# Two-part first query load, a later second query load, half of the first key products on GpSimd, and new engine orders in an attention-plus-MLP kernel

## The chip, the cores and the metric

The kernel runs on one core of one Trainium2 chip. The metric is the device time of one execution in microseconds (us). Three executions of the kernel before took 103.77, 103.62 and 103.83 us; their median is 103.77 us.

## What is computed

Four batches of four heads, 1088 tokens, head dimension 32: a linear attention with a degree-two polynomial sketch, followed by a two-layer MLP with a `h - tanh(h)` activation. The attention output is the MLP's input, 4352 tokens of 128 features.

```python
def phi(x):
    a = np.einsum('rd,bhsd->bhsr', S1, x)          # r = 8
    b = np.einsum('rd,bhsd->bhsr', S2, x)
    return np.einsum('bhsi,bhsj->bhsij', a, b).reshape(*x.shape[:-1], r * r)
q_p, k_p = (phi(q), phi(k))
kv = np.einsum('bhsf,bhsd->bhfd', k_p, v)
z = np.sum(k_p, axis=2)
num = np.einsum('bhsf,bhfd->bhsd', q_p, kv)
den = np.einsum('bhsf,bhf->bhs', q_p, z)[..., None] + 1e-06
x = (num / den) ...                                 # to (4352, 128)
h = x @ w_in                                        # d_ff = 2048
out = (h - np.tanh(h)) @ w_out
```

## The kernel before

Each batch's tokens stand in 34 columns of 32 tokens. The program records named operations; five lists in `ORDERS` say, word for word, in which order each engine (TensorE, ScalarE, VectorE, GpSimd, and SyncE, which issues nearly all loads and stores) runs them. `SESSIONS` says in which order the users of each PSUM bank follow each other, and each pair `a<b` in `GATES` makes operation a wait for operation b. Nothing is reordered at run time: an instruction that waits holds all that stands behind it on its engine.

**Attention, keys (batch b).** `kT` turns the raw keys in 32x32 blocks (VectorE, line 542), `kp` multiplies them with the sketch weights (TensorE, 553), `kab` turns the result back (VectorE, 559). `wk` are the products of the two sketches (573), cut by `KCUTS` into pieces for VectorE and GpSimd. For batch 0, `kap0` (ScalarE, 563) first copies one factor to PSUM, so that VectorE's pieces read one operand from there. `gram` (584), `gm` (590) and `fold` (593) give the key sums folded with S2: `fold0` needs `gm0` and `s2f` (532), and `wq0u` (ScalarE, 597) copies its result out. `sum` (609), `kvz` (619), `turn` (629), `ndw` (636) make the matrices that queries are weighed with.

**Attention, queries (chunk u).** There are five chunks: 12 and 22 columns of batch 0, and then one of 34 for each further batch. `qT` turns the raw queries (656), `qp` and `qpu0` multiply (679 for chunk 0, 700), `qab` copies them out (ScalarE 691 for chunk 0, VectorE 706), `au`, `dn`, `rd`, `an` (711 to 717) form the denominator and the scaled factor, `qm` the products (724, on VectorE and GpSimd), `qt` their turned form (731), `num` weighs them (TensorE, 746) and `x` writes the MLP's input xT (769).

**MLP.** Ten groups of 256 to 512 tokens. For each of 16 blocks of w_in a group has `h` (TensorE, 829 or 838), `t` = tanh (ScalarE, 832 or 841; three PSUM banks in turn, or pairs of banks in groups 7 to 9), and `o` (TensorE, 889 or 854), which accumulates tanh against w_out. The part without tanh is added as xT against `w_in @ w_out`, which is formed once: `wT` transposes w_in by DMA (SyncE, 782), `wp` multiplies (787), `whi`/`wlo` split it (791, 792), `lin` applies it (881). `out` turns a result (894) and SyncE stores it (901). Operation h17 is block 1 of group 1: 16 operations make a group.

**Casts.** `wic0` to `wic3` cast the four quarters of w_in (775; the last on GpSimd), `woc0` to `woc2` the parts of w_out (778, GpSimd).

**Filler.** TensorE's list also has matmuls whose result nobody reads: `~` (256 columns in a 32-wide strip, line 424), `*`, `!`, `$` (512 columns) and `^` (256 columns), line 416. `!` waits for `qab1`, `$` for `wqu0`.

Of the kernel before, what the change touches and what calls it, by code (L numbers as in the profile page):

```python
# [271 lines left out]
ORDERS = {
    "tensor": """
~52 sk ~17 kp0 sk2 *4 ^1 gram0 qp0 fold0 *2 ^1 qpu0 sum0.0 sum0.4 qp1 turn0 $2 num0.0 num0.1 !1 h0 h1 h2 o0 h3 o1 h4
o2 h5 o3 kp1 h6 h7 h8 h9 o4 h10 gram1 o5 h11 o6 h12 fold1 o7 h13 o8 h14 o9 h15 num1.0 num1.1 o10 o11 o12 h30 h22 h20
wp h19 h18 h32 h31 o13 o14 h47 o15 h24 lin0.whi h16 lin0.wlo h17 qp2 h42 h23 lin1.whi h25 lin1.wlo o16 o17 h21 o18 o19
h29 o20 h28 h27 o21 o22 o23 h26 o24 o25 h34 h39 o26 o27 h38 o28 h43 kp2 h33 o29 o30 h35 o31 h46 h45 gram2 lin2.whi h40
fold2 lin2.wlo sum1.0 h36 h44 o32 o33 o34 turn1 o35 h37 h41 o36 num2.0 num2.1 o37 o38 o39 o40 o41 o42 h51 h49 o43 o44
o45 o46 h48 o47 h53 h64 qp3 h50 h57 lin3.whi h52 lin3.wlo o48 h59 h54 o49 o50 h55 h65 o51 o52 o53 h63 h56 o54 h58 o55
h60 h62 o56 o57 h61 o58 h66 o59 h68 sum2.0 h67 h69 o60 turn2 h74 h70 o61 o62 h72 o63 h73 num3.0 num3.1 h76 lin4.whi  # L280
h71 lin4.wlo h78 h79 o64 o65 o66 h77 o67 o68 o69 h85 h75 h80 o70 kp3 h84 o71 h83 o72 h109 gram3 o73 h87 o74 fold3 h88
h101 o75 o76 o77 h82 o78 h81 h86 o79 h103 qp4 lin5.whi h91 lin5.wlo o80 o81 h90 o82 h89 o83 o84 h108 h94 o85 o86 o87
o88 h92 o89 o90 h93 h97 o91 o92 h95 h105 sum3.0 h98 h96 o93 o94 o95 turn3 h111 h100 h110 lin6.whi lin6.wlo o96 o97 o98
h99 h104 num4.0 num4.1 h102 h106 h107 o99 o100 h116 h112 h113 o101 o102 o103 h117 h114 o104 o105 h115 h119 h118 o106
o107 o108 o109 o110 o111 h123 h122 h121 h125 h120 lin7.whi h124 lin7.wlo h129 o112 o113 o114 h128 o115 h126 o116 o117
h127 o118 h130 o119 h135 h134 h131 o120 o121 o122 h133 o123 h132 h141 o124 o125 o126 o127 h140 h136 h137 h139 h138
lin8.whi lin8.wlo o128 o129 o130 o131 o132 h144 h145 h147 h146 o133 o134 h142 h143 h149 h148 o135 o136 h150 o137 o138
h152 o139 h151 o140 o141 h153 o142 o143 lin9.whi h154 h155 lin9.wlo o144 h157 h156 o145 o146 o147 o148 h158 o149 h159
o150 o151 o152 o153 o154 o155 o156 o157 o158 o159
""",  # L290
    "scalar": """
k0.1 s1 act0 kap0 wq0u qab0 wic0 kvz0 ndw0 wic1 wic2 x0.0 t0 t1 t2 t3 t4 t5 t6 t7 t8 t9 t10 t11 t12 t13 t14 t15 x1.0
x1.2 t30 t22 t20 t19 t32 t18 t31 t47 t24 t17 t16 t42 t23 t25 t21 t29 t28 t27 t26 t34 t39 t38 t43 t33 t46 t35 t45 t40
kvz1 t36 t44 ndw1 t37 t41 t51 t49 t48 t53 t64 t50 t57 t52 t59 t54 t55 t65 t63 t56 t58 t60 t62 t61 t66 t68 kvz2 t67 t69
t70 ndw2 t74 t73 t72 t76 t71 t78 t79 t77 t75 t80 t85 t84 t83 t109 t87 t88 t101 t82 t103 t81 t86 t91 t90 t89 t94 t108
t92 t93 t97 t95 t105 kvz3 t96 t98 ndw3 t111 t110 t99 t100 t104 t102 t107 t106 t112 t116 t114 t118 t122 t120 t124 t128
t126 t134 t130 t132 t140 t138 t136 t144 t146 t148 t142 t150 t152 t154 t156 t158 out9.1 st9
""",
    "vector": """
hm4 hm4.0 hm4.1 hm4.2 hm4.3 sel bmask hm2 kT0.2 wkm kT0.0 wq wq0 qT0.0 kab0 qT0.12 s2f gm0 wk0.0 wk0.8 wk0.16 au0 dn0  # L300
wqu0 rd0 an0 qm0.0 qt0.0 qt0.2 qab1 au1 dn1 rd1 an1 kT1.2 kT1.0 qm1.0 kab1 qt1.2 gm1 qt1.0 wqu1 wk1.0 whi wlo wk1.24
qT1.0 out0 qab2 kT2.2 dn2 rd2 kT2.0 kab2 out1 gm2 qt2.2 wqu2 qt2.0 wk2.0 wk2.24 x2.0 x2.2 qT2.0 out2 qab3 qT3.0 dn3
rd3 qt3.2 qt3.0 out3 x3.2 x3.0 kT3.0 kT3.2 kab3 gm3 wk3.0 wk3.24 wqu3 out4 qab4 dn4 rd4 qt4.0 out5 qt4.2 x4.0 x4.3
x4.2 out6 out7 out8 out9.0
""",
    "gpsimd": """
id0 id1 au1.0 kTz0 qTz0 vz1 identb au1.1 kTz1 wqz vz0 wk0.22 wk0.29 qm0.2 qTz1 wic3 woc0 qm1.2 woc1 woc2 wk1.30 wk1.12
au2 an2 qm2.2 qm2.0 wk2.30 au3 wk2.12 an3 qm3.2 qm3.0 wk3.12 au4 wk3.30 an4 qm4.0 qm4.2
# [684 lines left out]
```

## Time and profile before

| what | us |
|---|---|
| median of three executions | 103.77 |
| the profiled execution, as timed | 104.69 |
| its span, first to last instruction | 101.8 |
| TensorE busy | 93.5 (92% of the span) |
| ScalarE busy | 78.5 (77%) |
| VectorE busy | 54.8 (54%) |
| GpSimd busy | 34.7 (34%) |
| chain that ended last: share on TensorE | 68% |
| the same: VectorE, GpSimd, DMA | 13%, 7%, 4% |

The span is cut into instructions with their start and duration on each engine. "Idle before" names what an engine waited for. The chain that ended last is followed back from the last instruction, at each step to what released it. Matmuls overlap: one of 512 columns is recorded with 0.38 us, but six in a row take 1.46 us, so that the spacing of two starts, 0.216 us, and not the duration, is what one costs in a row.

### The profile page before, as it was taken

What the parts mean: (1) busy time and instruction counts of PE and PEld (TensorE: products, weight loads), DVE (VectorE), ACT (ScalarE), POOL (GpSimd) and SP (SyncE); (2) the same over time, 40 slices, a digit from 0 to 9 for tenths busy, and PEclk for the clock granted to TensorE, in tenths of its full rate; (3) what the DMA queues carried; (4) which work ended last, traced back from release to release, by engine and by line L of the source; (5) the groups of instructions that cost most, each with busy time, mean ns of one, the idle gap of its engine ahead of it and who ended that gap; (6) DMA issues with size and microseconds to landing.
All of it is one profiled execution on the core that took longest, in us unless ns stands there. A gap on an engine that the chain in (4) does not pass through costs nothing.

```text
span 101.8 us, 3175 instructions
## 1 busy us (share of the span) xinstructions
PE 93.5 (92%) x1358; PEld 48.7 (48%) x1370; DVE 54.8 (54%) x95; ACT 78.5 (77%) x156; POOL 34.7 (34%) x42
## 2 busy tenths in 40 slices
...
GB/s 57 362 246 278 348 336 160 283 114 241 6 243 221 10 189 139 0 78 182 90 72 181 65 6 0 0 144 36 10 40 37 6 0 79 76 0 58 65 51 100
DMA packets 25966, 11.74 MB, mean 115 GB/s; under 512 B 19808, under 2 KB 24416, under 8 KB 25952
## 3 DMA queue, kind: packets, MB, share of 16 engines
...
q10 hardware_dynamic: 328, 0.40, 1.4%
q8 instruction: 10, 0.16, 0.8%
...
HBM read 8.79 MB, written 2.23 MB: 108 GB/s over the span
## 4 chain that ended last, share of the span: by engine, by line
PE 68%; DVE 13%; POOL 7%; DMA 4%; issue 2%; SPq 1%; ACT 1%; DVEq 0%; POOLq 0%
PE ps L889 23%; PE ps L838 16%; PE ps L829 8%; PE ps L746 6%; POOL qp L724 4%; DMA qraw<-in_q_dram 4%; PE ps L881 3%; DVE qpT L731 2%; PE ps L700 2%; PE ps L609 2%; DVE qab L706 2%; PE ps L553 2%; PE ps L854 2%; DVE wk L573 2%; POOL wk L573 1%
## 5 line engine op out<-in xcount | busy, mean ns | idle before, releaser
L841 ACT ACTIVATE tt<-ps 128x512 bf16<-128x512 f32 (+2 forms) x112 | 52.5, 552 | 8.4 <-PE ps L838 4.2
L889 PE MATMUL ps<-tt,w_out 128*128 128x512 bf16 (+3 forms) x141 | 39.0, 355 | 0.5 <-ACT tt L841 0.3
L838 PE MATMUL ps<-xT,w_in 128*128 128x512 bf16 (+2 forms) x107 | 32.7, 353 | 2.0 <-ACT tt L841 0.7
L889 PEld LDWEIGHTS ps<-tt,w_out 128*128 128x128 bf16 x144 | 13.9, 98 | 12.8 <-issue 1.4
L832 ACT ACTIVATE tt<-ps 128x1024 bf16<-128x1024 f32 (+2 forms) x24 | 18.4, 860 | 0.5
L838 PEld LDWEIGHTS ps<-xT,w_in 128*128 128x128 bf16 x112 | 9.9, 97 | 16.9 <-ACT tt L841 11.0
L724 POOL TENSOR_TENSOR qp<-an,qab 128x1152 f32<-128x1152 f32 (+2 forms) x8 | 15.4, 1925 | 3.6 <-DVE an L717 3.1
L731 DVE STREAM_TRANSPOSE qpT<-qp 128x1152 f32<-128x1152 f32 (+2 forms) x10 | 11.2, 1128 | 8.6 <-POOL qp L724 8.6
L894 DVE STREAM_TRANSPOSE osb<-ps 128x512 f32<-128x512 f32 (+3 forms) x9 | 5.9, 657 | 17.5 <-PE ps L889 17.0
L573 POOL TENSOR_TENSOR wk<-kab 128x384 f32<-128x384 f32 (+2 forms) x8 | 9.0, 1126 | 18.6 <-PE ps L889 18.1
L829 PE MATMUL ps<-xT,w_in 128*128 128x512 bf16 (+2 forms) x48 | 12.1, 335 | 0.1
L746 PE MATMUL ps<-qpT,ndw 32*32 32x288 f32 (+4 forms) x320 | 6.9, 352 | 0.4 <-DVE qpT L731 0.3
L829 PEld LDWEIGHTS ps<-xT,w_in 128*128 128x128 bf16 x48 | 4.5, 98 | 4.6 <-ACT tt L832 1.2
L542 DVE STREAM_TRANSPOSE kT<-kraw 128x512 f32<-128x512 f32 (+1 forms) x8 | 5.6, 718 | 0.8 <-DMA kraw<-in_k_dram 0.8
L656 DVE STREAM_TRANSPOSE qT<-qraw 128x1088 f32<-128x1088 f32 (+2 forms) x5 | 5.3, 1065 | 1.1 <-DMA qraw<-in_q_dram 1.1
L706 DVE STREAM_TRANSPOSE qab<-ps 128x1152 f32<-128x1152 f32 (+1 forms) x4 | 5.1, 1272 | 1.4 <-PE ps L700 1.4
L711 POOL TENSOR_TENSOR au<-qab 128x288 f32<-128x288 f32 x3 | 2.4, 790 | 9.9 <-DVE qab L706 7.0
L769 DVE CAST xT<-ps 128x576 bf16<-128x576 f32 (+2 forms) x7 | 4.4, 684 | 2.5 <-PE ps L746 2.5
L746 PEld LDWEIGHTS ps<-qpT,ndw 32*32 32x32 f32 x320 | 4.0, 103 | 3.2 <-DVE qpT L731 2.0
L609 PE MATMUL ps<-wk,vx 128*32 128x64 f32 x288 | 4.8, 220 | 0.0
L609 PEld LDWEIGHTS ps<-wk,vx 128*32 128x32 f32 x288 | 4.2, 110 | 0.7 <-issue 0.7
L559 DVE STREAM_TRANSPOSE kab<-ps 128x576 f32<-128x576 f32 x4 | 3.1, 769 | 2.7 <-PE ps L553 2.7
...
## 6 DMA issues: line engine op xcount, KB each, us to landing
...
vx<-in_v_dram SPq DMA_DIRECT2D x8, 128.0 KB, 3.3
...
```

The costliest lines, as they stand in the source:

```text
L573: P.op(f"wk{b}.{n0}", eng, (dve if eng == "vector" else pool)(64 * n), lambda e, n0=n0, n1=n1, n=n, a_=a_: e.tensor_tensor(out=wk[0][:, n0 ...
L609: ins = e.matmul(ps[32 * h:32 * h + 32, SB, 0:64], vx[i][:, h, t, :], wk[0][:, 4 * t + h, :], start=(t == 0), stop=(t == 8), tile_position ...
L706: P.op(f"qab{u}", "vector", dve(32 * n), lambda e: e.transpose(out=qab[ui][:, 0:n, :].rearrange("p (h t) x -> p h t x", h=H), in_=ps[:, b0 ...
L724: P.op(f"qm{u}.{h0}", eng, (pool if eng == "gpsimd" else dve)(64 * (n1 - n0)), lambda e, n0=n0, n1=n1, b_=b_: e.tensor_tensor(out=qp[ui][: ...
L731: P.op(f"qt{u}.{h0}", "vector", dve(64 * (n1 - n0)), lambda e, n0=n0, n1=n1: e.transpose(out=qpT[ui][:, n0:n1, :, :].rearrange("p n y j -> ...
L746: ins = e.matmul(ps[32 * h:32 * h + 32, ct, 0:32 * own[ct]], ndw[i][32 * ct:32 * ct + 32, y, 32 * h:32 * h + 32], qpT[ui][32 * ct:32 * ct ...
L829: P.op(f"h{s + y}", "tensor", pe(n), lambda e, jb=jb, b0=b0, y=y: e.matmul(ps[:, b0 + y, 0:n], w_in[:, 128 * (jb + y):128 * (jb + y) + 128 ...
L832: P.op(f"t{s}", "scalar", act(2 * n), lambda e, ts=ts, b0=b0: e.activation(out=tt[:, ts:ts + 2, 0:n], in_=ps[:, b0:b0 + 2, 0:n], func=AF.T ...
L838: P.op(f"h{s}", "tensor", pe(n), lambda e, jb=jb, bk=bk: e.matmul(ps[:, bk, 0:n], w_in[:, 128 * jb:128 * jb + 128], xT[:, t0:t0 + n], star ...
L841: P.op(f"t{s}", "scalar", act(n), lambda e, ts=ts, bk=bk: e.activation(out=tt[:, ts, 0:n], in_=ps[:, bk, 0:n], func=AF.Tanh, scale=-1.0), ...
L889: P.op(f"o{slot + jb}", "tensor", pe(n), lambda e, jb=jb, ts=ts: e.matmul(acc[:, 0:n], w_out[:, jb, :], tt[:, ts, 0:n], start=late and jb ...
L894: P.op(f"out{g}", "vector", dve(n), lambda e: e.transpose(out=osb[u][:, 0:n], in_=acc[:, 0:n]), r=ka, w=[("osb", u)], prio=when)
```

## The change

- The first batch's queries are loaded in two parts (columns 0 to 11, then 12 to 33) instead of three. The first part is issued right behind the keys, the second behind the values and ahead of w_in.
- `KCUTS` for batch 0 gives VectorE three pieces of 6 (18 of 36) and GpSimd two of 9 (18 of 36); before, VectorE had 22 and GpSimd 14.
- `s2f` is four small ScalarE operations (line 530 of the new file) instead of one on VectorE.
- All five orders, the bank sessions and the gates are new.

```diff
-KCUTS = ((('vector', 0, 8), ('gpsimd', 22, 29), ('vector', 8, 16), ('gpsimd', 29, 36), ('vector', 16, 22)), (('gpsimd', 12, 24), ('vector', 0, 12), ('vector', 24, 30), ('gpsimd', 30, 36)), (('gpsimd', 12, 24), ('vector', 0, 12), ('vector', 24, 30), ('gpsimd', 30, 36)), (('gpsimd', 12, 24), ('vector', 0, 12), ('vector', 24, 30), ('gpsimd', 30, 36)))
+KCUTS = ((('vector', 0, 6), ('gpsimd', 18, 27), ('vector', 6, 12), ('gpsimd', 27, 36), ('vector', 12, 18)), (('gpsimd', 12, 24), ('vector', 0, 12), ('vector', 24, 30), ('gpsimd', 30, 36)), (('gpsimd', 12, 24), ('vector', 0, 12), ('vector', 24, 30), ('gpsimd', 30, 36)), (('gpsimd', 12, 24), ('vector', 0, 12), ('vector', 24, 30), ('gpsimd', 30, 36)))
...
-WENG = ()
+WENG = ('s2f',)
 SKB = 6
 WOC = ((0, 4), (4, 8), (8, 16))
+Q0 = ((0, 384), (384, 1088))
...
     "tensor": """
-~52 sk ~17 kp0 sk2 *4 ^1 gram0 qp0 fold0 *2 ^1 qpu0 sum0.0 sum0.4 qp1 turn0 $2 num0.0 num0.1 !1 h0 h1 h2 o0 h3 o1 h4
+~43 *1 sk ~4 sk2 ~16 kp0 *5 gram0 qp0 fold0 *1 ^1 qpu0 sum0.0 sum0.4 *2 turn0 qp1 $1 num0.0 num0.1 !1 h1 h11 h9 h10 h5 h0
...
     "gpsimd": """
-id0 id1 au1.0 kTz0 qTz0 vz1 identb au1.1 kTz1 wqz vz0 wk0.22 wk0.29 qm0.2 qTz1 wic3 woc0 qm1.2 woc1 woc2 wk1.30 wk1.12
-au2 an2 qm2.2 qm2.0 wk2.30 au3 wk2.12 an3 qm3.2 qm3.0 wk3.12 au4 wk3.30 an4 qm4.0 qm4.2
+qTz0 kTz0 id0 id1 au1.0 vz1 kTz1 vz0 qTz1 wk0.27 wk0.18 au1.1 wqz qm0.2 wic3 woc0 qm1.2 woc1 woc2 wk1.30 wk1.12 au2
+an2 qm2.0 qm2.2 wk2.30 wk2.12 au3 an3 qm3.0 qm3.2 wk3.30 identb wk3.12 au4 an4 qm4.2 qm4.0
...
 GATES = """
-id0<hm4.3 kTz0<hm4.3 kTz1<qT0.0 vz0<sel au1.0<bmask au1.1<bmask wqz<kp0 qTz0<hm4 qTz1<wq0 vz1<wq v1.0<o11 v1.1<h25
+id1<hm4.2 kTz1<qT0.0 vz0<sk2 au1.0<kT0.2 au1.1<qpu0 wqz<wqu0 s1<hm4.0 k0.0<kTz0 v1.0<t16 v1.1<kT2.0 v1.2<dn2 v1.3<t17
...
-    load_q(0, 0, 256, L + 2, 0)
+    for x, (lo, hi) in enumerate(Q0):
+        load_q(0, lo, hi, L + 2 + 3 * x, x)
     load_v(0, "sync", L + 3)
     load_w_in(0, L + 5)
     load_w_in(1, L + 6)
-    load_q(0, 256, 640, L + 8, 1)
     load_w_in(2, L + 8.5)
     load_w_in(3, L + 9)
-    load_q(0, 640, S, L + 10, 2)
```

VectorE before, from the turn of batch 0's key sketches (`kab0`) to the products of chunk 0 (`qm0.0`); the row with 704 columns is the second part of batch 0's queries being turned:

```order
L559 STREAM_TRANSPOSE kab<-ps 128x18x2x16
L656 STREAM_TRANSPOSE qT<-qraw 128x704
L532 TENSOR_TENSOR s2f<-ps,bmask 128x128
L590 TENSOR_TENSOR gm<-ps,bmask 128x32
L573 TENSOR_TENSOR wk<-ps,kab 128x512 x2
L573 TENSOR_TENSOR wk<-ps,kab 128x384
L711 TENSOR_TENSOR au<-qab,ps 128x12x8
L713 TENSOR_REDUCE dn<-au 128x12
L599 TENSOR_REDUCE wq<-ps 128x8
L715 RECIPROCAL rd<-dn 128x12
L717 TENSOR_TENSOR an<-ps,rd 128x96
L724 TENSOR_TENSOR qp<-an,ps 128x384
```

The same stretch of VectorE now:

```order
L560 STREAM_TRANSPOSE kab<-ps 128x18x2x16
L446 TENSOR_REDUCE bmask<-ident 128x4
L526 COPY wq<-ps 128x4x16
L591 TENSOR_TENSOR gm<-ps,bmask 128x32
L574 TENSOR_TENSOR wk<-ps,kab 128x384 x3
L712 TENSOR_TENSOR au<-qab,ps 128x12x8
L714 TENSOR_REDUCE dn<-au 128x12
L600 TENSOR_REDUCE wq<-ps 128x8
L716 RECIPROCAL rd<-dn 128x12
L718 TENSOR_TENSOR an<-ps,rd 128x96
L657 STREAM_TRANSPOSE qT<-qraw 128x704
L725 TENSOR_TENSOR qp<-an,ps 128x384
```

The 704-column turn went from ahead of `gm0` to between `an0` and `qm0.0`, `s2f` left the engine, two small operations came in, and the key products shrank from 1408 to 1152 elements a partition.

SyncE's opening before (kraw are keys, qraw queries, vx values; 128x1088 is a whole batch):

```order
L918 DMA s<-in_S_dram 8x4x32
L466 DMA kraw<-in_k_dram 128x576
L472 DMA qraw<-in_q_dram 128x384
L472 DMA qraw<-in_q_dram 128x256
L472 DMA qraw<-in_q_dram 128x448
L489 DMA vx<-in_v_dram 32x4x288 x2
L489 DMA vx<-in_v_dram 32x4x256 x2
L495 DMA w_in_f<-in_moe_w_in_dram 128x512 x4
L500 DMA w_out_f<-in_moe_w_out_dram 128x4x128
L466 DMA kraw<-in_k_dram 128x1088
L500 DMA w_out_f<-in_moe_w_out_dram 128x4x128
L500 DMA w_out_f<-in_moe_w_out_dram 128x8x128
```

And now:

```order
L919 DMA s<-in_S_dram 8x4x32
L467 DMA kraw<-in_k_dram 128x576
L473 DMA qraw<-in_q_dram 128x384
L490 DMA vx<-in_v_dram 32x4x256 x2
L490 DMA vx<-in_v_dram 32x4x288 x2
L473 DMA qraw<-in_q_dram 128x704
L496 DMA w_in_f<-in_moe_w_in_dram 128x512 x4
L467 DMA kraw<-in_k_dram 128x1088
L501 DMA w_out_f<-in_moe_w_out_dram 128x4x128 x2
L501 DMA w_out_f<-in_moe_w_out_dram 128x8x128
L473 DMA qraw<-in_q_dram 128x1088
L783 DMA_TRANSPOSE w_inT<-w_in 128x16x128
```

The columns that chunk 0 needs now come in one load instead of two; the rest of batch 0's queries moved behind the values; batch 1's keys and queries moved ahead (the queries stood behind the transposing DMA `wT`).

VectorE before, around batch 1's keys and chunk 1, from `an1` on:

```order
L717 TENSOR_TENSOR an<-qab,rd 128x192
L542 STREAM_TRANSPOSE kT<-kraw 128x2x8x32
L542 STREAM_TRANSPOSE kT<-kraw 128x2x9x32
L724 TENSOR_TENSOR qp<-an,qab 128x768
L559 STREAM_TRANSPOSE kab<-ps 128x18x2x16
L731 STREAM_TRANSPOSE qpT<-qp 128x768
L590 TENSOR_TENSOR gm<-ps,bmask 128x32
L731 STREAM_TRANSPOSE qpT<-qp 128x768
L599 TENSOR_REDUCE wq<-ps 128x8
L573 TENSOR_TENSOR wk<-kab 128x768
```

The same stretch now:

```order
L718 TENSOR_TENSOR an<-qab,rd 128x192
L725 TENSOR_TENSOR qp<-an,qab 128x768
L543 STREAM_TRANSPOSE kT<-kraw 128x2x9x32
L543 STREAM_TRANSPOSE kT<-kraw 128x2x8x32
L732 STREAM_TRANSPOSE qpT<-qp 128x768 x2
L560 STREAM_TRANSPOSE kab<-ps 128x18x2x16
L574 TENSOR_TENSOR wk<-kab 128x384
L574 TENSOR_TENSOR wk<-kab 128x768
L657 STREAM_TRANSPOSE qT<-qraw 128x1088
L591 TENSOR_TENSOR gm<-ps,bmask 128x32
```

Chunk 1's products and their turns went ahead of batch 1's `kab1`, and `gm1` went behind both `wk1` pieces and the turn of batch 1's queries.

82 lines of the change are left out of this document (41 added, 41 removed).

## The prediction

> **What bounds the kernel now.** First the busy time by stage. I cut the span where the MLP starts, where its first group ends, and where the last attention work ends.
>
> ```profile
> core 0: us, PE busy (x) PEld busy (x) DVE busy (x) ACT busy (x) POOL busy (x), PEclk, DMA share, GB/s
> 0.00:14.30 14.30, 11.72 (x311) 7.88 (x314) 10.35 (x31) 5.16 (x11) 6.43 (x21) 1.00 0.91 268
> 14.30:23.20 8.90, 8.04 (x129) 3.63 (x129) 7.20 (x13) 7.00 (x18) 3.70 (x3) 1.00 0.95 200
> 23.20:78.00 54.80, 53.08 (x787) 26.11 (x795) 33.69 (x46) 46.40 (x101) 24.55 (x18) 1.00 0.38 92
> 78.00:98.70 20.70, 20.61 (x134) 11.08 (x132) 3.26 (x6) 19.70 (x28) 0.00 (x0) 1.00 0.24 38
> PE ps L838 <- ACT tt L841: 0.4, 2, 0.2
> PE ps L746 <- DVE qpT L731: 0.3, 1, 0.3
> ```
>
> From 23.2 us on TensorE lacks 1.72 + 0.09 = 1.8 us of being busy all the time, and the change takes no matmul out of it. (The last two lines, of the waits from 23.2 to 98.7, name 0.7 us of it.) The third stage can give at most 1.8 us. The rest is a delay: whatever makes the MLP start or its first group end earlier moves the end as far, unless later waits grow. What sets that start is read in the chain that ended last:
>
> ```profile
> 2.06 4.20 DMA qraw<-in_q_dram
> 6.35 0.58 DVE qT L656
> 6.93 0.66 DVE kab L559
> 8.66 1.66 DVE wk L573 x3
> 10.32 0.17 DVE au L711
> 11.08 0.27 DVE an L717
> 11.37 0.56 DVE qp L724
> ```
>
> Loads, then VectorE without a pause: `qT0.0` waits for the queries until 6.35, and `kab0` stands behind it. TensorE's timeline shows what these hold:
>
> ```profile
> 0.77 2.96 PE L424 MATMUL ps<-const-bfloat16-1.0 128*32 128x256 bf16 x52 [0.77 <-PEq L978]
> 4.04 0.73 PE L424 MATMUL ps<-const-bfloat16-1.0 128*32 128x256 bf16 x17
> 5.07 0.72 PE L553 MATMUL ps<-kT,wkm 64*32 64x288 f32 x16 [0.31 <-DVE kT L542]
> 7.65 0.38 PE L584 MATMUL ps<-kab 128*32 128x32 f32 x18 [0.43 <-DVE kab L559]
> 8.71 0.41 PE L593 MATMUL ps<-gm,s2f 128*128 128x32 f32 x2 [0.19 <-DVE gm L590]
> 14.34 0.66 PE L838 MATMUL ps<-xT,w_in 128*128 128x384 bf16 x3 [0.57 <-ACT xT L769]
> 21.36 1.25 PE L746 MATMUL ps<-qpT,ndw 32*32 32x192 f32 x64
> 81.29 1.46 PE L889 MATMUL ps<-tt,w_out 128*128 128x512 bf16 x6
> ```
>
> **Term 1, the start of the MLP: -0.6 us.** These rows give the prices:
>
> ```profile
> qraw<-in_q_dram SPq DMA_DIRECT2D x1, 192.0 KB, 3.2
> qraw<-in_q_dram SPq DMA_DIRECT2D x1, 128.0 KB, 4.2
> 7.52 0.87 DVE L656 STREAM_TRANSPOSE qT<-qraw 128x704 f32<-128x704 f32 x1
> 7.63 0.40 ACT L563 COPY ps<-kab 128x288 f32<-128x288 f32 x1 [4.33 <-DVE kab L559]
> 9.16 0.19 ACT L597 COPY wq<-ps 128x32 f32<-128x32 f32 x1 [1.13 <-PE ps L593]
> L573 POOL TENSOR_TENSOR wk<-kab 128x384 f32<-128x384 f32 x3 | 2.5, 847 | 6.8 <-PE ps L889 6.7
> L573 POOL TENSOR_TENSOR wk<-kab 128x448 f32<-128x448 f32 x2 | 1.9, 958 | 0.2 <-POOL vx L450 0.2
> ```
>
> The new first query load is the 192 KB size, in that load's place: there by about 4.8 instead of 6.26 (2.06 + 4.20). `kT0.0` is done at 5.0 (`kp0` starts on it at 5.07, as now), `qT0.0` (0.58) and one small operation fit before `kp0` ends at 5.79, so `kab0` starts at 5.83 instead of 6.85 and ends at 6.57. Behind it TensorE has five fillers of 0.216 (six 512-column matmuls start within 1.46 - 0.38): `gram0` at 6.9 to 7.3. `gm0` (about 0.2) ends at 7.5. `s2f` on ScalarE follows `kap0` (6.6 to 7.0). The trace has no such operation; four of them cost from 0.4 (starts 0.08 apart, as the next copy stands behind the 0.19 row) to 0.8 (four times 0.19). I take 0.5, so 7.5; at 0.8 it would cost 0.1, as `fold0` comes only behind `qp0`, at 7.7. From `fold0`'s start to `au0` the chain takes 10.24 - 8.71 = 1.53 now. `qab0` moves ahead of `wq0u` and runs beside `fold0`, so 1.3 remain: `au0` at 9.0. VectorE's three products of 384, each started some 0.47 after the other, end at 8.9 and so hide. GpSimd's two of 576 cost, by the slope of the two rows above (111 ns for 64), 1.18 each, from 6.7 to 9.1, ahead of `qm0.2`'s start at 10.2: hidden; 0.3 more each would cost 0.1 at most. `au0` is 1.24 earlier. But the 704-column `qT` now stands between `an0` and `qm0.0`: `an0` at 9.84, that turn from 10.0 with 0.79 to the next start, `qm0.0` at 10.8 against 11.37. So 0.6 of 1.24 is left. First `h` at 13.75. `wic1` now stands between `x0.0` and the first tanh; it fills the time in which ScalarE waits for the first `h`.
>
> **Term 2, the first group: -0.6 us.** Chunk 1's `num1.0` (21.36) ends this stage.
>
> ```profile
> 14.71 2.41 ACT L841 ACTIVATE tt<-ps 128x384 bf16<-128x384 f32 x6 [0.43 <-PE ps L838]
> 17.99 4.08 ACT L841 ACTIVATE tt<-ps 128x384 bf16<-128x384 f32 x10 [0.86 <-PE ps L838]
> 15.27 0.36 DVE L717 TENSOR_TENSOR an<-qab,rd 128x192 f32<-128x192 f32 x1
> 15.54 1.36 DVE L542 STREAM_TRANSPOSE kT<-kraw 128x512 f32<-128x512 f32 x2
> 16.83 1.20 DVE L724 TENSOR_TENSOR qp<-an,qab 128x768 f32<-128x768 f32 x1
> 17.96 0.77 DVE L559 STREAM_TRANSPOSE kab<-ps 128x576 f32<-128x576 f32 x1
> 19.71 0.97 DVE L731 STREAM_TRANSPOSE qpT<-qp 128x768 f32<-128x768 f32 x1
> 15.71 1.51 POOL L724 TENSOR_TENSOR qp<-an,qab 128x768 f32<-128x768 f32 x1 [1.43 <-DVE an L717]
> L573 DVE TENSOR_TENSOR wk<-kab 128x768 f32<-128x768 f32 x3 | 2.8, 935 | 0.0
> ```
>
> ScalarE idles 0.86 there, because `kp1` stood early in TensorE's list and waited for the keys' turn. Now nine `h` come first, so tanh runs at its pace: from 14.1, 16 in (4.08 - 0.50) / 9 = 0.40 each, and the last `h` can go in about 19.7. VectorE: `an1` at 14.7 to 15.0, `qm1.0` 1.2, two `kT` 1.29, two `qt` 1.8, `kab1` 0.77: 20.1. `num1.0` writes the banks that `kab1` reads: 20.1 instead of 21.36. That is -1.2 in all, 0.6 beyond term 1. `woc0` comes later (batch 1's keys are loaded ahead of it, about 15.1), but `o0` is not due before 16.7.
>
> **Term 3, a new wait at `fold1`: +0.5.** VectorE's `qm1.0` took 1.20 while GpSimd's 1.51 ran (until 17.22); products of the same 768 elements took 0.935 with GpSimd idle. So two such operations side by side lose 0.26 here. The change sets batch 1's four products together, at about 20: VectorE's 384 and 768 beside GpSimd's, which before waited until 25.9. `qT1.0` and `gm1` stand behind them on VectorE, and `fold1` waits for `gm1` on TensorE with all MLP work behind it. VectorE: 20.1 + 1.3 + 1.2 = 22.6, TensorE is at `fold1` at about 23.0. If GpSimd's first (0.85) is wholly added, `fold1` waits 0.5; without that, nothing. The ends are 0 and 0.9 (both 0.85 and some of the next); I take 0.5. The Trainium skill, "SBUF — State Buffer", section "SBUF: two separate sides", says that VectorE with two SBUF inputs and GpSimd share a port pair as an exclusive lock, and the loser waits for the whole instruction. The 1.20 against 0.935 agrees, and batch 0's pieces (one PSUM operand) show no such loss. By the rule taken fully term 3 would be 0.9.
>
> **Term 4, later waits: -0.6.** Of the 1.8 us the 0.7 named can go: the 0.3 at `num` (GpSimd's `wk2.12` now runs ahead of `au3`, not between `au3` and `an3`) and the 0.4 at tanh. Ends: -1.8 and +0.5, since every order here is new. I keep -0.6.
>
> **Sum:** -0.6 - 0.6 + 0.5 - 0.6 = -1.3 us. The profiled execution took 104.69 with a span of 101.8; its 2.9 outside the span and the 3.1 after the last matmul stay. Its span would be 100.5. The median of the runs lies 0.92 below the profiled time, so 103.77 - 1.3 = **102.5 us**.
>
> **The rivals.**
>
> *The second query load is late.* `qm0.0` now stands behind `qT0.12`, whose load is behind the values. Bytes ahead of w_in are the same as before, so it should land by 9.9, 0.1 before it is wanted. But the 128 KB load took 4.2 us where the 192 KB one before it took 3.2. A landing at 10.8 costs 0.8: 103.3.
>
> *The middle gives it back.* Term 3 at 0.9 and term 4 at +0.3, ScalarE (19.70 of the last 20.70) being nearly as tight as TensorE: terms 1 and 2 cancel, 103.77.
>
> *Slower: w_in's transpose arrives after its turn.*
>
> ```profile
> w_inT<-w_in SPq DMA_TRANSPOSE x1, 5.8
> ```
>
> It was issued at 13.7; now it waits for `h2`, the eighth `h`, at 16.3, behind the load of batch 1's queries (544 KB), and lands at 22.1 if it takes 5.8 again. `wp` and everything behind it on TensorE want it at about 23.9. The gain is gone when it lands 1.3 later than that, 25.2, or 8.9 after issue. At 10 it would be 104.9. Against it: the 5.8 already had w_out loads beside it.
>
> *Slower: TensorE's rate does not rise in time.* 52 fillers took 2.96 (0.05 apart), the 17 after 4.0 us 0.73 (0.02 apart), though the page's granted clock reads 1.00. The early filler is cut from 52 and 17 to 43, 4 and 16, and one of 512. If `kp0`, `gram0` and `fold0` ran at half that rate, 0.72 + 0.38 + 0.41 = 1.5 is added: 104.0. The Trainium skill, "TensorE: Matmul & The Clock Gate", "What's actually happening", has such a step, after about 3.4 us of sustained work. By its rule the new list still fills that time.
>
> **How the numbers follow.** Forecast 102.5 with its own range 101.8 to 103.1: 0.61. Late load: 0.12. Given back: 0.14. Late transpose: 0.08. Low rate: 0.05. A measurement of this kernel tells about 0.2% (0.2 us) from no change. Faster: 0.61 + 0.12 + 0.04 of the given-back case = 0.77; same 0.10; slower 0.08 + 0.05 = 0.13. The range goes from 101.6 (term 3 at 0, term 4 at -1.0) to 103.6.
>
> **What would show it.** Right: `kab0` near 5.8, `au0` near 9.0, first `h` near 13.75, `num1.0` near 20.1, an idle of 0.3 to 0.9 at `fold1`, less idle than 1.8 on TensorE behind. Wrong: `qT` of 704 columns waiting for a load, `wp` waiting for a DMA, fillers still 0.05 apart after 4.5 us, or `num1.0` behind 20.8.

## The result, and the profile after

| what | before | after |
|---|---|---|
| the profiled execution, as timed | 104.69 us | 102.34 us |
| its span | 101.8 us | 100.6 us |
| 20 executions of each: median | 104.04 us | 104.34 us |
| 20 executions of each: lowest and highest | 103.08, 106.24 us | 102.27, 104.73 us |
| ratio of the shorter executions, 95% interval | | 0.9878 [0.9841, 0.9916] |

The executions after fall into two groups, 5 at 102.27 to 102.88 us and 15 at 104.01 to 104.73; the ratio compares the shorter group with the like of before, so that by it the kernel is 1.2% faster, while the median of all 20 is 0.3 us above that of before. The sum of the prediction, made against a profiled execution, belongs to the shorter group; where the longer one comes from is what most of the experiments are about.

First the busy time by stage of the kernel after, cut at the same events as the rows of before (start of the MLP, end of its first group, end of the last attention work):

```profile
core 0: us, PE busy (x) PEld busy (x) DVE busy (x) ACT busy (x) POOL busy (x), PEclk, DMA share, GB/s
0.00:14.30 14.30, 13.22 (x310) 7.82 (x311) 10.27 (x31) 5.50 (x15) 5.98 (x19) 1.00 0.90 273
14.30:22.50 8.20, 7.67 (x108) 3.17 (x108) 8.06 (x12) 7.34 (x19) 5.81 (x6) 1.00 0.87 221
22.50:77.00 54.50, 54.17 (x818) 27.19 (x816) 33.17 (x47) 46.91 (x102) 23.85 (x18) 1.00 0.39 93
77.00:97.40 20.40, 20.35 (x134) 11.24 (x131) 3.30 (x7) 19.32 (x27) 0.00 (x0) 1.00 0.21 33
```

From the end of the first group on TensorE lacked 1.81 us of being busy; now it lacks 0.33 + 0.05 = 0.38. The first stage is as long as before. TensorE's waits over the whole span (what it waited for, us in total, times, longest) say the same, three of them where this list of before counts seventeen:

```profile
PE ps L425 <- PEq L978: 0.8, 1, 0.8
PE ps L747 <- DVE qpT L732: 0.3, 1, 0.3
PE ps L839 <- ACT tt L842: 0.3, 1, 0.3
```

The opening on VectorE, in its timeline (start, duration, instruction, idle before it):

```profile
5.16 0.58 DVE L657 STREAM_TRANSPOSE qT<-qraw 128x384 f32<-128x384 f32 x1
6.09 0.78 DVE L560 STREAM_TRANSPOSE kab<-ps 128x576 f32<-128x576 f32 x1 [0.24 <-PE ps L554]
...
9.38 0.26 DVE L712 TENSOR_TENSOR au<-qab,ps 128x96 f32<-128x96 f32 x1 [0.27 <-PE ps L680]
...
10.24 0.26 DVE L718 TENSOR_TENSOR an<-ps,rd 128x96 f32<-128x96 f32 x1
10.41 0.90 DVE L657 STREAM_TRANSPOSE qT<-qraw 128x704 f32<-128x704 f32 x1
11.24 0.52 DVE L725 TENSOR_TENSOR qp<-an,ps 128x384 f32<-128x384 f32 x1
```

`qT0.0` no longer waits for the queries, `au0` starts 0.86 earlier than before, and `qm0.0` (the last row) only 0.13 earlier: the 704-column turn between them takes the rest. ScalarE's and TensorE's timelines show the two other places:

```profile
6.91 0.40 ACT L564 COPY ps<-kab 128x288 f32<-128x288 f32 x1 [3.62 <-DVE kab L560]
7.25 0.81 ACT L530 ACTIVATE s2f<-ps,bmask 128x32 f32<-128x32 f32 x4
```

```profile
8.11 0.41 PE L594 MATMUL ps<-gm,s2f 128*128 128x32 f32 x2
...
14.21 0.66 PE L839 MATMUL ps<-xT,w_in 128*128 128x384 bf16 x3
...
20.68 1.25 PE L747 MATMUL ps<-qpT,ndw 32*32 32x192 f32 x64
...
23.05 0.38 PE L585 MATMUL ps<-kab 128*32 128x32 f32 x18
...
23.71 0.41 PE L594 MATMUL ps<-gm,s2f 128*128 128x32 f32 x2
```

`fold0` starts (8.11) as the four `s2f` end (7.25 + 0.81); the first `h` stands at 14.21, `num1.0` at 20.68, and `gram1` and `fold1`, which stood at 19.18 and 20.15, now come behind it, with no wait ahead of them.

The two kernels against each other, each operation by its start in the trace and, from the first `h` on, by its distance from the first `h`:

| operation | before | after |
|---|---|---|
| first `h` (from the span's start) | 14.34 | 14.21 |
| `num1.0`, behind the first `h` | 7.02 | 6.47 |
| `qp2` | 12.75 | 12.58 |
| `x4.0` | 63.20 | 62.35 |
| the last `o` | 84.00 | 82.82 |

### The profile page after: what moved, and what is told of

Same layout as the page of the kernel before. It is cut to its first block, busy times and chain, and to the rows that moved or that the text cites. A ratio compares the mean times of both kernels' runs of the same rounds, so it can differ in the third digit from the quotient of the medians.

```text
span 100.6 us, 3180 instructions
## 1 busy us (share of the span) xinstructions
PE 95.4 (95%) x1365; PEld 49.4 (49%) x1365; DVE 55.1 (55%) x94; ACT 79.3 (79%) x160; POOL 35.6 (35%) x42
## 4 chain that ended last, share of the span: by engine, by line
PE 81%; POOL 6%; DVE 5%; ACT 4%; issue 1%; POOLq 0%
PE ps L890 25%; PE ps L839 18%; PE ps L830 8%; PE ps L747 7%; POOL qp L725 4%; PE ps L610 3%; PE ps L425 3%; PE ps L701 3%; PE ps L882 3%; ACT tt L842 2%; PE ps L855 2%; PE ps L554 2%; PE ps L417 2%; DVE qab L707 1%; DVE qpT L732 1%; PE ps L788 1%
## 5 line engine op out<-in xcount | busy, mean ns | idle before, releaser
L890 PE MATMUL ps<-tt,w_out 128*128 128x512 bf16 (+3 forms) x144 | 40.0, 356 | 0.0
L839 PE MATMUL ps<-xT,w_in 128*128 128x512 bf16 (+2 forms) x112 | 35.2, 355 | 0.6 <-ACT tt L842 0.3
L839 PEld LDWEIGHTS ps<-xT,w_in 128*128 128x128 bf16 x112 | 10.6, 97 | 17.2 <-ACT tt L842 10.7
L574 POOL TENSOR_TENSOR wk<-kab 128x384 f32<-128x384 f32 (+2 forms) x8 | 10.2, 1280 | 14.0 <-PE ps L890 5.6
L830 PE MATMUL ps<-xT,w_in 128*128 128x512 bf16 (+2 forms) x48 | 11.8, 335 | 0.0
L830 PEld LDWEIGHTS ps<-xT,w_in 128*128 128x128 bf16 x48 | 4.5, 98 | 4.5 <-ACT tt L833 1.2
L574 DVE TENSOR_TENSOR wk<-kab 128x384 f32<-128x384 f32 (+1 forms) x6 | 5.0, 865 | 0.0
L610 PE MATMUL ps<-wk,vx 128*32 128x64 f32 x288 | 4.9, 220 | 0.0
L610 PEld LDWEIGHTS ps<-wk,vx 128*32 128x32 f32 x288 | 4.2, 110 | 0.7 <-DMA vx<-in_v_dram 0.4
```

Source lines behind the costliest of these rows:

```text
L574: P.op(f"wk{b}.{n0}", eng, (dve if eng == "vector" else pool)(64 * n), lambda e, n0=n0, n1=n1, n=n, a_=a_: e.tensor_tensor(out=wk[0][:, n0 ...
L610: ins = e.matmul(ps[32 * h:32 * h + 32, SB, 0:64], vx[i][:, h, t, :], wk[0][:, 4 * t + h, :], start=(t == 0), stop=(t == 8), tile_position ...
L830: P.op(f"h{s + y}", "tensor", pe(n), lambda e, jb=jb, b0=b0, y=y: e.matmul(ps[:, b0 + y, 0:n], w_in[:, 128 * (jb + y):128 * (jb + y) + 128 ...
L839: P.op(f"h{s}", "tensor", pe(n), lambda e, jb=jb, bk=bk: e.matmul(ps[:, bk, 0:n], w_in[:, 128 * jb:128 * jb + 128], xT[:, t0:t0 + n], star ...
L890: P.op(f"o{slot + jb}", "tensor", pe(n), lambda e, jb=jb, ts=ts: e.matmul(acc[:, 0:n], w_out[:, jb, :], tt[:, ts, 0:n], start=late and jb ...
```

## The experiments

All times below are medians with the lowest and highest execution. "The new opening list" is TensorE's list of the kernel after up to `gram0`, "the old one" that of the kernel before.

**e1: nothing changed.**

> The changed kernel once more, nothing edited, as the yardstick of the others on this chip. Every theory expects a ratio to the kernel before of 0.984 to 0.992 and a span of about 100.6 us; if the transposed w_in comes late in an execution, its profile shows TensorE waiting for it at the product of w_in and w_out (line 788), with up to 2 us of idle time.

Measured: 104.2 us (102.32 to 104.6, 12 executions), again in two groups: 3 up to 102.68, 9 from 103.78 on. The profiled execution is one of the longer ones, 104.6 us, and in it TensorE never waits for the transpose. Its TensorE timeline:

```profile
4.32 0.40 PE L425 MATMUL ps<-const-bfloat16-1.0 128*32 128x256 bf16 x4
4.65 0.63 PE L512 MATMUL ps<-s,sel 16*128 16x32 f32 x2
5.21 1.04 PE L425 MATMUL ps<-const-bfloat16-1.0 128*32 128x256 bf16 x16
6.18 1.21 PE L554 MATMUL ps<-kT,wkm 64*32 64x288 f32 x16
7.33 2.19 PE L417 MATMUL ps<-const-bfloat16-1.0 128*128 128x512 bf16 x5
9.45 0.38 PE L585 MATMUL ps<-kab 128*32 128x32 f32 x18
```

and the same rows of the shorter execution above:

```profile
4.15 0.29 PE L425 MATMUL ps<-const-bfloat16-1.0 128*32 128x256 bf16 x4
4.38 0.40 PE L512 MATMUL ps<-s,sel 16*128 16x32 f32 x2
4.71 0.62 PE L425 MATMUL ps<-const-bfloat16-1.0 128*32 128x256 bf16 x16
5.26 0.72 PE L554 MATMUL ps<-kT,wkm 64*32 64x288 f32 x16
5.91 1.26 PE L417 MATMUL ps<-const-bfloat16-1.0 128*128 128x512 bf16 x5
7.11 0.38 PE L585 MATMUL ps<-kab 128*32 128x32 f32 x18
```

Instruction for instruction the longer one is slower by a factor of 1.4 to 1.7 until `gram0`, which then takes 0.38 in both and stands 2.3 later; the first `h` stands 2.0 later (16.22), and from there all is alike: the last `o` comes 82.82 behind the first `h` in both. The trace also records when TensorE's granted clock changes; these are the changes, in us from the span's start:

```
after           rises at  3.92
e1_same         rises at  9.27
before          rises at  3.62
```

So these two executions differ by when the clock rises, and behind the first `h` by nothing. That the two groups of times differ by this is inferred: of the executions with the new opening list that were profiled, the other two with late rises (e2 at 9.45, e7 at 9.35) had their first `h` at 16.31 and 16.27 as well. The page's row of the granted clock does not show this: its first entry is 9 for both.

**e2: `wT` no longer waits for `h2`.** It tells the rival "w_in's transpose arrives late" from the rest.

```diff
-qm0.2<sum0.4 qm1.2<h13 wT<h2 wk1.30<o3 ...
+qm0.2<sum0.4 qm1.2<h13 wk1.30<o3 ...
```

> The gate of w_in's transposing DMA on the eighth h is taken away, so it is issued when the last cast of w_in ends, at about 14.7 us instead of 17.0. Theory of the late transpose (it lands at 23.1 in the profile, TensorE wants it at 24.4, and now and then it comes later): the landing moves to about 21, and the longest times of the changed kernel (up to 104.7) go; the best ones stay at 102.3 to 102.9. Rival (the spread has nothing to do with it): the times lie as for the unedited kernel, within 0.2 us at both ends.

Measured: 103.98 us (102.36 to 104.3, 12 executions), the same two groups: 4 up to 103.03, 8 from 103.85 on. The profiled one is long (104.3), its clock rises at 9.45 and its last `o` stands 82.80 behind its first `h`, as in e1. The transpose is not what is late.

**e3: `s2f` as one VectorE operation again.**

```diff
-WENG = ('s2f',)
+WENG = ()
-k0.1 s1 act0 kap0 s2f.0 s2f.1 s2f.3 s2f.2 qab0 wq0u ...
+k0.1 s1 act0 kap0 qab0 wq0u ...
-... wq0 kab0 bmask wq gm0 ...
+... wq0 kab0 bmask s2f wq gm0 ...
```

> s2f goes back to one operation on VectorE, where that engine waits for gram0. Theory of the mis-sized first term (the four ScalarE operations took 0.81 us instead of 0.5, and fold0 waits for them): fold0 moves from 8.11 to about 7.9, au0 and the first h 0.2 to 0.4 us earlier, the time 0.2 to 0.4 us lower. Rival (something else releases fold0 or au0): first h within 0.1 us, time the same.

Measured: 103.11 us (102.08 to 104.64, 6 executions, three of them up to 102.39); profiled 102.39. On VectorE one operation does it:

```profile
7.28 0.29 DVE L533 TENSOR_TENSOR s2f<-ps,bmask 128x128 f32<-128x128 f32 x1
```

`kp0` stood 0.21 later in this execution (5.47), and `fold0` still stood at 8.12 and the first `h` at 14.18, which are the rival's numbers. Measured from `kp0`, `fold0` comes 2.65 behind it instead of 2.85: with this opening list, `s2f` on ScalarE cost 0.2 at `fold0`, which the later `kp0` hides here.

**e4: only the loads and `qT0.12`, in the kernel before.**

```diff
+Q0 = ((0, 384), (384, 1088))
...
-    load_q(0, 0, 256, L + 2, 0)
+    for x, (lo, hi) in enumerate(Q0):
+        load_q(0, lo, hi, L + 2 + 3 * x, x)
...
-    load_q(0, 256, 640, L + 8, 1)
...
-    load_q(0, 640, S, L + 10, 2)
...
-... wq wq0 qT0.0 kab0 qT0.12 s2f gm0 wk0.0 wk0.8 wk0.16 au0 dn0 wqu0 rd0 an0 qm0.0 ...
+... qT0.0 wq0 kab0 wq s2f gm0 wk0.0 wk0.8 wk0.16 au0 dn0 wqu0 rd0 an0 qT0.12 qm0.0 ...
-s2 k0.0 q0.1 q0.0 q0.2 v0.1 ...
+s2 k0.0 q0.0 v0.1 v0.0 v0.2 v0.3 q0.1 ...
```

> The kernel before with the change's loading of batch 0's queries alone (two parts, the second behind the values), and on VectorE the 704-column turn between an0 and qm0.0; all else as before. Theory of a small first term (what the early queries give is taken back by the turn that moved into the chain): kab0 about 0.8 us earlier, first h 0.1 to 0.5 us earlier, time 0.1 to 0.5 us lower. Rival (the loads are the whole gain): 1.0 us or more lower.

Measured: 104.91 us (104.24 to 105.82, 6 executions), ratio 1.01 [1.0063, 1.0138]: slower. On VectorE `kab0` comes 0.70 earlier than before (6.15) and `au0` 0.54 earlier (9.70), but `qm0.0`, behind the 704-column turn, 0.19 later (11.56): the turn takes back all that the load gives. TensorE has two new waits, and GpSimd's timeline shows where the first comes from:

```profile
PE ps L610 <- POOL wk L574: 0.4, 1, 0.4
PE ps L701 <- DVE qT L657: 0.3, 1, 0.3
```

```profile
7.10 0.20 POOL L458 MEMSET vx<- 64x128 f32 x1 [3.89 <-DVE wq L526]
8.61 2.00 POOL L574 TENSOR_TENSOR wk<-kab 128x448 f32<-128x448 f32 x2
```

The edit also moved `wq` on VectorE from ahead of `qT0.0` (4.94 before) to behind `kab0` (6.85), and the gate `vz1<wq` of the old list holds GpSimd until then. Its key products start at 8.61 instead of 7.79, and the sums (L610) wait for them. Chunk 1's `qp` (L701) waits for the late turn. The first `h` stands at 14.87, 0.53 later than before. In the profiled execution, the longest of the six (105.82), some 1.9 us more than before also lie behind the last `o`; why was not seen. The numbers are neither theory's, and the run measures the loads together with a late GpSimd: what the split alone does to the time stays open, and which other part of the change makes it pay was not run by itself.

**e5: the old opening list in the kernel after.**

```diff
-~43 *1 sk ~4 sk2 ~16 kp0 *5 gram0 ...
+~52 sk ~17 kp0 sk2 *4 ^1 gram0 ...
-... vz0<sk2 ...
+... vz0<sel ...
```

> The kernel after, with the opening list of TensorE of the kernel before: 52 strips, sk, 17 strips, kp0, sk2, four fillers and a short one, gram0 (and GpSimd's vz0 behind sel, as before). Theory R (which filler stands around sk and sk2 decides in how many executions the fast rate comes by 4.5 us and not at about 9.3): most times lie at 102.2 to 103.0 and their median near 102.7; kp0 starts by 5.4 and takes 0.72, first h by 14.4. Rival C (the spread has nothing to do with TensorE's list; it comes from the loads or from the chip): most times stay at 104.0 to 104.7, as in the unedited kernel, median near 104.2.

**e6: the new opening list in the kernel before** (the same line, the other way round).

> The kernel before with the changed kernel's opening list on TensorE alone (43 strips, one filler, sk, 4 strips, sk2, 16 strips, kp0, five fillers, gram0). Theory R: most executions get the fast rate only at about 9.3 us; kp0 takes 1.2, the first products of the MLP start some 1.5 to 2 us later than in before, and the median is 105.2 to 106.5. Rival C: the median is that of before within 0.3 (103.8 to 104.3).

Measured: e5 102.89 us (5 of 6 executions at 102.32 to 103.06, one at 107.04), ratio 0.9895 [0.9843, 0.9948]. e6 104.31 us (103.42 to 105.59): 6 of 12 executions lie at 104.76 or more, against 5 of 23 of the kernel before beside it. The times of e5 are as theory R expected. e6 has more long executions, which these counts cannot tell from chance with any certainty, and not the median that theory R named: by the median alone it lies at the edge of rival C's. The long execution of e5 happened to be the profiled one, and in it the clock rose only at 16.68 us, so the old list can miss too. Its last `o` still stands 82.81 behind the first `h` (18.71).

**e8: e5 with `s2f` on VectorE** (both edits above).

> As e5_old_filler, with s2f as one operation on VectorE (as in before) in place of four on ScalarE. Theory S (s2f on ScalarE holds fold0 by 0.2 to 0.3, and VectorE has room for it): fold0 at 7.8 to 8.0, first h 0.1 to 0.2 earlier than in e5_old_filler, time 102.0 to 102.6. Rival N (the one operation on VectorE takes what the four on ScalarE took): as e5_old_filler within 0.15.

Measured: 103.29 us (102.19 to 103.77, 12 executions). None is long by 2 us, but most are some 0.6 longer than e5's, against both theories. In the profiled one (103.31) the clock rose at 4.66. `fold0` stood at 8.12 and `au0` at 9.39; e10 below, with `s2f` on ScalarE behind the same opening list, has 8.11 and 9.38. So behind the old list the move of `s2f` costs nothing at `fold0`, as rival N says. Yet the first `h` stood at 14.96:

```profile
11.48 0.52 PE L701 MATMUL ps<-qT,wq 32*32 32x192 f32 x6
12.54 0.60 PE L701 MATMUL ps<-qT,wq 32*32 32x192 f32 x26 [0.54 <-issue]
```

TensorE stopped for 0.54 in the middle of `qp1`, six records into it, on nothing that the profile shows. This comes again in e12 and is taken up there.

**e7: batch 1's `gram1` and `fold1` back ahead of `num1.0`, in the kernel after.**

```diff
-... o4 o5 o6 o7 h15 num1.0 num1.1 o8 ... h22 gram1 h20 h36 fold1 o13 ...
+... o4 o5 gram1 o6 o7 h15 fold1 num1.0 num1.1 o8 ... h22 h20 h36 o13 ...
-... kab1 wk1.24 wk1.0 qT1.0 gm1 wqu1 ...
+... kab1 gm1 wk1.24 wk1.0 qT1.0 wqu1 ...
```

> The kernel after with batch 1's gram1 and fold1 back ahead of num1.0 on TensorE (and gm1 ahead of batch 1's products on VectorE). Theory M (term 2's gain is work that was moved behind num1.0, so it is no gain of the end): num1.0 starts 6.85 to 7.1 after the first h of the MLP instead of 6.47, qp2 still 12.4 to 12.7 after it (12.58 in after), and what follows stands to the first h as in after within 0.2. Rival G (an earlier num1.0 is worth its whole advance, term 2 as predicted): qp2 and everything behind it lie 0.4 to 0.6 later against the first h, and so does the end.

Measured: 110.34 us (109.4 to 110.9, 4 executions). The edit missed that `num1` needs the bank that `wqu1` reads, and `wqu1` stood behind three VectorE operations:

```profile
27.27 1.92 PE L747 MATMUL ps<-qpT,ndw 32*32 32x192 f32 x64 [3.92 <-DVE wq L600]
29.12 1.78 PE L890 MATMUL ps<-tt,w_out 128*128 128x384 bf16 x5
```

It says nothing of its question. But the wait shows the clock again: it fell at 26.42 and rose at 33.25, this time long enough to be read on the page (tenths of full speed in 40 slices of the span):

```profile
PEclk9999999998559999999999999999999999999998
```

**e9: the same question, with `wqu1` ahead of the products too**, and e5's opening list.

```diff
-... kab1 wk1.24 wk1.0 qT1.0 gm1 wqu1 ...
+... kab1 gm1 wqu1 wk1.24 wk1.0 qT1.0 ...
```

> e5_old_filler with batch 1's gram1 and fold1 ahead of num1.0 on TensorE, and gm1 and wqu1 ahead of batch 1's products on VectorE, so that num1.0 does not wait for wqu1 as in e7_fold1_back. Theory M (what term 2 gained beyond term 1 is work moved behind num1.0): num1.0 starts 6.85 to 7.2 after the first h of the MLP instead of 6.47, qp2 still 12.4 to 12.8 after it (12.58 in after); time within 0.3 of e5_old_filler's 102.3 to 103.0. Rival G (an earlier num1.0 is worth its whole advance): qp2 and the end 0.4 to 0.6 later against the first h, time 0.4 to 0.6 longer.

Measured: 103.31 us (103.2 to 104.74, 10 executions). `num1.0` stands 7.54 behind the first `h`, `qp2` 13.55 and the last `o` 83.77, some 0.95 more than in after: neither theory's numbers. The trace says what of it is work and what is waiting:

```profile
20.27 0.38 PE L585 MATMUL ps<-kab 128*32 128x32 f32 x18
...
21.67 1.25 PE L747 MATMUL ps<-qpT,ndw 32*32 32x192 f32 x64 [0.28 <-DVE wq L600]
...
24.50 0.34 PE L839 MATMUL ps<-xT,w_in 128*128 128x384 bf16 x1 [0.26 <-ACT tt L842]
```

Between the first `h` and `qp2` TensorE does the same work in after and in e9, so the 0.97 by which `qp2` is later is all waiting: for `kab1` ahead of `gram1`, for `wqu1` ahead of `num1.0`, and for tanh behind it. Behind `num1.0` those two products wait for nobody. That is what the order of after is worth against this one; an earlier `num1.0` of itself was not separated from it.

**e10: `o37` and `o38` ahead of `num2.0`, in e5**, at the one wait of 0.3 that after has behind its opening.

```diff
-... h44 o36 h39 num2.0 num2.1 o37 o38 o39 o40 ...
+... h44 o36 h39 o37 o38 num2.0 num2.1 o39 o40 ...
```

> e5_old_filler with o37 and o38 ahead of num2.0 on TensorE, where in after TensorE waits 0.3 to 0.46 for the turn of the query products. Theory I (from the first group on, TensorE's idle is time of the kernel): that wait falls to 0.15 or less, everything behind lies 0.2 to 0.35 earlier against the first h, time 0.2 to 0.35 below e5_old_filler's (median 102.4 to 102.7). Rival A (ScalarE, or the later first h behind num2.1, takes it back): x4.0 stands to the first h as in after within 0.1, and the time is unchanged within 0.2.

Measured: 102.75 us (102.18 to 103.37, 6 executions), ratio 0.989 [0.9844, 0.9937]; profiled 102.18, the shortest of all profiled executions. The wait is gone; `x4.0` stands 62.16 and the last `o` 82.63 behind the first `h`, both 0.19 earlier. Theory I, a hair below its numbers; the time itself cannot tell 0.19 from none in so few executions.

**e11: the first queries in three parts again, in e5.**

```diff
-Q0 = ((0, 384), (384, 1088))
+Q0 = ((0, 256), (256, 640), (640, 1088))
-... kab0 bmask wq gm0 wk0.6 wk0.12 wk0.0 au0 dn0 wqu0 rd0 an0 qT0.12 qm0.0 ...
+... kab0 qT0.12 bmask wq gm0 wk0.6 wk0.12 wk0.0 au0 dn0 wqu0 rd0 an0 qm0.0 ...
-s2 k0.0 q0.0 v0.2 v0.3 v0.1 v0.0 q0.1 wi0 ...
+s2 k0.0 q0.1 q0.0 q0.2 v0.2 v0.3 v0.1 v0.0 wi0 ...
```

> e5_old_filler with the first queries loaded in three parts in the order of the kernel before (qT0.0 needs two of them) and qT0.12 back ahead of gm0. Theory as measured (the two-part load brings kab0 and au0 0.8 earlier, but qT0.12 between an0 and qm0.0 gives 0.8 of it back): au0 about 0.8 to 1.2 later than the 9.38 of after, first h at most 0.3 later (14.2 to 14.5), time at most 0.3 longer than e5_old_filler's (102.7 to 103.2). As predicted in term 1: first h 0.5 to 0.8 later (14.7 to 15.0) and the time as much longer (103.2 to 103.6).

Measured: 103.22 us (102.37 to 105.0, 12 executions). `au0` at 10.71, first `h` at 15.08, 0.87 later than in after: beyond both. But its one large new wait is not the load's:

```profile
PE ps L594 <- ACT s2f L530: 1.2, 1, 1.2
```

`bmask` now stood behind `qT0.12`, so the four `s2f` began at 8.56 instead of 7.25 and `fold0` waited for them. Inconclusive as to the loads: it measures them together with a late `s2f`.

**e12: a third opening list, in the kernel after**, with `sk2` behind `kp0` and the first 43 strips kept.

```diff
-~43 *1 sk ~4 sk2 ~16 kp0 *5 gram0 ...
+~43 *1 sk ~17 kp0 *4 sk2 *1 gram0 ...
-... vz0<sk2 ...
+... vz0<sel ...
```

> The kernel after with another opening list of TensorE: 43 strips, one filler, sk, 17 strips, kp0, four fillers, sk2, one filler, gram0: only sk2 is moved, from ahead of kp0 to behind it, so that the two small products sk and sk2 do not fall into the same 3.4 us. Theory R (the rate rises at the end of a stretch of 3.4 us with little pause in it, at a phase that differs by execution; sk and sk2 both count as pause): most times at 102.2 to 103.0, at most one in four at 104.0 to 104.8, kp0 takes 0.72. Rival F (what helped in e5_old_filler is the larger number of strips ahead of sk): most times stay at 104.0 to 104.8.

Measured: 104.34 us (103.53 to 105.81, 12 executions): the times are not theory R's. The profiled execution, the shortest, had its clock rise at 3.56 and `kp0` at 0.72, as R wants, and then this in `qp1`:

```profile
11.56 0.54 PE L701 MATMUL ps<-qT,wq 32*32 32x192 f32 x13
12.99 0.57 PE L701 MATMUL ps<-qT,wq 32*32 32x192 f32 x19 [0.88 <-issue]
```

The stop is e8's again, 0.88 long. Counted over TensorE's whole list it falls behind the same number of matmul records, the 219th here and the 220th in e8, though the two lists differ ahead of it. The list of DMA queues in the microsecond from 10 to 11 has a packet of a queue that is named "instruction":

```profile
q8 instruction: 1, 0.02, 6.5%
```

In after that packet came in the microsecond from 9 to 10, at 9.27; here it came at 10.52, in e8 at 10.30. In e8 and e12 TensorE went on 1.2 and 1.4 us after the packet's end. After itself has a small stop of the same kind: 0.23 between two starts in `qp1`, behind the 221st record, 1.4 us after its packet ended at 10.38. In e1 and e2 the packet came late too (10.39 and 10.53), but that record came only at 13.7 and 13.8, and nothing stopped. So it looks as if TensorE waited for its own instructions; no run tested that. Why the longer executions of e12 are longer was not seen, and whether its list raises the clock in time more often stays open.

## Why the prediction came out as it did

The profiled time was 102.34 us against 102.5 predicted, and the span fell by 1.3 us, as summed. That this is so close is luck: term 1 gave 0.5 less than predicted and term 4 gave 0.4 more. Of the signs named for being right only the last came, less idle time behind the first group; `kab0` (6.09), `au0` (9.38), the first `h` (14.21) and `num1.0` (20.68) all came later than named, and `fold1` waited for nothing. And the times of most executions are those of a rival.

**Term 1 (-0.6), mis-sized: -0.13.** The mechanism holds step by step: the queries are no longer waited for, `kab0`, `gm0`, `fold0`, `au0` come earlier in a chain, and the 704-column turn takes 0.83 of it back (10.41 to 11.24; 0.79 was predicted). The chain itself gained 0.86 at `au0` and not 1.24. Two sizes failed. `kab0` came at 6.09 instead of 5.83, since `kp0` started 0.19 later than before instead of as before, with no wait ahead of it: TensorE was still at the filler of its new list. And `s2f` on ScalarE took 0.81, the upper of its two bounds, behind a `kap0` that was itself 0.3 late, so that `fold0` started at 8.11 instead of 7.7; e3 shows 0.2 of that by its absence, with the new opening list (with the old one, e8 against e10, there is none of it).

**Term 2 (-0.6) and term 3 (+0.5): -0.17 together, -0.1 predicted.** `num1.0` came 0.55 nearer to the first `h`, where 0.6 was predicted. The giving back is real too, but the step "VectorE and GpSimd side by side make `fold1` wait" failed. Two such products side by side do lose time, as the timelines of VectorE and GpSimd show:

```profile
20.20 2.08 DVE L574 TENSOR_TENSOR wk<-kab 128x384 f32<-128x384 f32 x2
```

```profile
20.42 3.23 POOL L574 TENSOR_TENSOR wk<-kab 128x384 f32<-128x384 f32 x2 [0.17 <-POOL w_out L779]
```

2.08 on VectorE against 0.55 + 0.94 for a 384 and a 768 alone; that agrees with the rule that the prediction cited from the Trainium skill, "SBUF — State Buffer", section "SBUF: two separate sides", though not with its full size. But nothing waited for it: `fold1` stood at 23.71 with no idle ahead of it, because `gram1` and `fold1` had been moved behind `num1.0`. What gave back the advance is work that was moved out of the stage and paid behind it: `gram1` and `fold1`, and by TensorE's lists `o8` and `o9` too. In before these four take 0.31, 0.14, 0.17 and 0.16 us ahead of `num1.0`, 0.78 together, more than the 0.55 by which it came nearer. From the first `h` to `qp2` both lists hold the same numbers of each product, and there the gain is the 0.17.

**Term 4 (-0.6), mis-sized: -1.0.** From `qp2` to the last `o` TensorE needs 82.82 - 12.58 = 70.24 instead of 71.25. Of the waits that the prediction named, that of `num` went at `num3.0`, and a like one came at `num2.0`; the tanh waits behind the first group went. The value was held to the 0.7 of named waits; the gain came as well from idle time that no named wait covers, which the term had in its bound of 1.8 only. (The list of waits of before from 23.2 us on has 0.8 us of it, as "issue": idle time with no releaser seen.) e10 shows that such idle is time of the kernel: 0.19 of the 0.3 at `num2.0` came out at the end.

**The rival "TensorE's rate does not rise in time"** (0.05, slower, 104.0) fits the times of 15 of the 20 executions after, 104.01 to 104.73, and it was argued away with a step that failed: "By its rule the new list still fills that time." The list fills the time, and yet the clock rose late. The records of the clock bound when it rises:

- It rises and falls on a grid. The stretches at full clock last 98.99, 95.57, 92.16 and 88.75 us in the runs above, and 17.07 in e7, all multiples of 3.41. The start of the grid differs by execution. That agrees with the Trainium skill, "TensorE: Matmul & The Clock Gate", section "What's actually happening": a window of 3413 ns that runs freely.
- How much of a stretch TensorE's records cover does not decide it alone. These are stretches of 3.41 us of that grid, worked out from TensorE's records and the changes of the clock:

| run | stretch | TensorE busy | of it `sk`, `sk2` | the clock at its end |
|---|---|---|---|---|
| e12 | 0.15 to 3.56 | 2.79 | none | rises |
| before | 0.21 to 3.62 | 2.85 | none | rises |
| e3 | 1.05 to 4.46 | 3.41 | `sk`, 0.60 | rises |
| e7 | 26.42 to 29.83 | 2.56 | none | stays low |
| e1 | 2.44 to 5.85 | 3.41 | both, 1.23 | stays low |
| e5 | 3.03 to 6.44 | 3.29 | `sk`, 0.57 | stays low |
| e5 | 6.44 to 9.85 | 3.08 | `sk2`, 0.63 | stays low |
| e5 | 9.85 to 13.27 | 3.41 | none | stays low |
| e5 | 13.27 to 16.68 | 3.08 | none | rises |

- Without `sk` or `sk2` in it, 2.56 of 3.41 (75%, e7) left the clock low and 2.79 (82%, e12) raised it. In e1 `sk` and `sk2`, each a small product of 16 rows, count as busy by their records; the other records cover 2.46 of that stretch, 72%. So it fits that these two count as pauses. e2 and e7 have a like stretch (2.62 to 6.04, 2.53 to 5.94) that left the clock low.
- e5 shows that this cannot be all. Its first stretch holds 2.79 without `sk`, as much as raised the clock in e12, and the one from 9.85 holds neither of the two and no pause. What fills that one is mostly the query products of chunk 0 (1.65) and `fold0` (0.64). Either these count for little too, or something else counts; no run separates the two.

In the old list `sk2` stands behind `kp0`, some 2 us or more behind `sk`, so that fewer phases put both into one early stretch; in the new one they stand 0.9 apart ahead of `kp0`. That this is why the new list is late more often is inferred and not shown, and e12, which moved `sk2` behind `kp0`, did not bring the short times back. A rise at 9.27 or 9.45 instead of 3.92 put the first `h` 2.0 or 2.1 us later, more than the whole sum of 1.3.

By count, with the new list 16 of 50 executions (after, e1, e2, e3) lie below 103.8 us, and with the old one in the same kernel (e5, e8, e10) 23 of 24; e9 and e11, which have the old list and other edits besides, have 8 of 10 and 10 of 12. The two lists were run on different chips, though: e1 to e4 on one, e5 to e8 on a second, e9 to e12 on a third. The kernel before had medians of 103.97, 103.98 and 103.96 on them, but the kernel after was not run beside e5, e8 or e10, so the count alone does not exclude the chip.

The other differences between the profiled executions of the changed kernel lie in the opening too. Behind the first `h` it runs alike in every profiled execution that kept its orders there:

| run | first `h` | the last `o` behind it | time |
|---|---|---|---|
| after | 14.21 | 82.82 | 102.34 |
| e3 | 14.18 | 82.78 | 102.39 |
| e8 (TensorE stops in `qp1`) | 14.96 | 82.79 | 103.31 |
| e11 (`s2f` late) | 15.08 | 82.75 | 103.34 |
| e12 (TensorE stops in `qp1`) | 15.37 | 82.80 | 103.53 |
| e1 (clock rises at 9.27) | 16.22 | 82.82 | 104.6 |
| e5 (clock rises at 16.68) | 18.71 | 82.81 | 107.04 |

So the time is the first `h` plus 88.0 to 88.4 us, and what decided each of these runs lies ahead of it.

The other rivals did not come: `qT0.12` waited for no load, and `wp` had its transpose (e2). The shortest medians of all executions are those of e10 and e5, the changed kernel with the old opening list: 102.75 and 102.89 us, against 104.34 after and 104.04 before. In the ratio of the shorter executions they are no better than after: 0.989 and 0.9895 against 0.9878.
